# Attention output rows: from wide rows with a sum to narrow rows in four column groups

## The chip, the cores and the metric

One Trainium2 chip, one of its cores. The metric is the device time of one execution in microseconds. The time before is 189.49 us, the median of three runs (189.31 to 189.62).

## What is computed

One token (a vector x of 512) goes through an attention block with a cache and through a small MLP, and a scalar gate mixes the two. Cut to what matters:

```python
q = (x @ wq)                                   # 512 -> 32 heads of 128
s = einsum(q, k_cache) * 128 ** -0.5           # 32 heads, 4096 cached keys each
p = softmax(s)
o = einsum(p, v_cache)                         # 32 heads of 128
a = o.reshape(1, 1, 4096) @ wo                 # 4096 -> 512
b = square(relu(x @ w1 + b1)) @ w2 + b2        # 512 -> 1376 -> 512
g = sigmoid((x * gate_w).sum())
out = g * a + (1 - g) * b                      # 512 numbers, bf16
```

The caches of keys and values are 32 MB each, wq and wo 4 MB each. All inputs are bf16.

## The kernel before, in words

**Loads.** SyncE (SP) issues almost all loads, from one list in program order: wq (lines 247 and 248), the keys and values in eight pieces each of 4 MB for four heads (`load_k`, `load_v`, lines 255 to 290), w1 and w2 in between, and last wo. A load into a buffer that is used again first waits for the engines that read the buffer. wo comes in four loads (line 293), by rows `TS = [0, 20, 28, 31, 32]`: rows 0 to 19, 20 to 27, 28 to 30 and row 31 (a "row" t here is 128 rows of the matrix wo, one on each partition, 512 columns). Each load has a semaphore of its own. After them SP waits for the result (line 295) and issues the store (line 296).

**Heads.** For each piece of keys, POOL and VectorE (DVE) form products of keys and query for a part of the keys (lines 313, 680) and DVE sums them (lines 689, 695); for the other part TensorE (PE) transposes keys (line 427), ScalarE (ACT) copies the transposes (line 341) and PE forms the scores (line 441). The softmax runs on ACT (line 358), and PE multiplies by the values (line 470) into the PSUM bank `pO`. The result is copied to `pvf` (line 364, the last one line 739 on DVE), and line 479 extracts the heads into columns 288 to 415 of the bank `pX`.

**MLP.** It runs during the first piece. Its bias is put into the result rows `accs` (line 520), its output rows go to `pO` with four rows of partial sums (line 528), which are copied to `pvf` (line 380) and summed into `accs` (line 535), all long before the end.

**The end.** After the last piece, `regroup` (line 541) brings the attention result to one column per row of wo, and DVE copies it to `o2` (line 744). Then `attn_rows(c)` (line 546) runs for the four loads of wo. The result of 512 numbers lies in `accs` (line 165): two rows of 128 numbers for even column blocks (partitions 32 and 33 of the bank `pX`) and two for odd ones (partitions 0 and 1). Rows 0 to 15 of wo are wide: one matmul of 512 columns each, to partition 0, 32, 64 or 96 of `pO`, so that four partial sums arise (line 551). DVE copies these to `pvf` (line 746), and `wide_rows` (line 566) sums them into `accs`, after the first load's rows and before the second's. Rows 16 to 31 are narrow: four matmuls of 128 columns each (line 557). Which of the two partitions of a pair a matmul adds to is chosen by its stationary operand of two columns, one of which is zero; for that, `o2p` holds each column of `o2` with a zero column on either side, and `pick2` a column of the selection with zeros beside it. `busy` (line 573) issues filler matmuls whose result nobody reads. At the end DVE copies one half of the result to `ob` (line 748) and ACT the other (line 385), and SP stores two rows of 256 numbers.

Of the kernel before, what the change touches and what calls it, by code (L numbers as in the profile page):

```python
# [5 lines left out]
def bass_gated_mix__gqa_block_cached__dense_activation_squared_relu__decode_kernel(  # L6
# [14 lines left out]
    fp32 = mybir.dt.float32  # L21
    i32 = mybir.dt.int32
    bf16 = mybir.dt.bfloat16
    ALU = mybir.AluOpType
    ACT = mybir.ActivationFunctionType
    AX = mybir.AxisListType

    NH = 32
# [39 lines left out]

    TS = [0, 20, 28, 31, 32]
    NW = len(TS) - 1  # L70
    WW = 16


    k_p = A_k_cache.rearrange("a h (q b) d -> (a h q) (b d)", b=NB)
# [2 lines left out]
    wo_v = A_wo.rearrange("(p t) n -> p (t n)", t=32)  # L77
    w1_v = B_w1.rearrange("(p t) n -> p (t n)", t=4)
    w2_v = B_w2[0:F0, :].rearrange("(p g) n -> p (g n)", g=FG)
    out_v = out[0, 0, :].rearrange("(j p) -> j p", p=256)  # L80
    w2_x = B_w2[F1:F, :].rearrange("(q t) n -> q (t n)", t=TX)

    ctx = ExitStack()
    with ctx:
        def sb(name, shape, dt):
            return ctx.enter_context(nc.sbuf_tensor(name, shape, dt))
# [4 lines left out]
        def sem(name):  # L91
            return ctx.enter_context(nc.semaphore(name))
# [8 lines left out]
        wo_sb = WO.rearrange("p (t n) -> p t n", t=32)  # L101
        kT = sb("kT", [128, NR, TC * 128], bf16)
# [9 lines left out]
        grow = sb("grow", [1, DM], bf16)  # L112
        b1r = sb("b1r", [1, F], bf16)

        ob = kT[:, 1, 0:256]
        xcol = sb("xcol", [128, 4], bf16)
        sel = sb("sel", [NH, 4, 128], bf16)
        oT = sb("oT", [NH, 128], bf16)
        o2p = sb("o2p", [128, NH, 3], bf16)
        o2 = o2p[:, :, 1]  # L120
        ident = sb("ident", [128, 128], bf16)
        identf = sb("identf", [128, 128], fp32)
        pick = sb("pick", [128, 4, 60], fp32)
        pvf = sb("pvf", [112, 512], fp32)
# [20 lines left out]
        b2r = Kt[0:1, 2, 14 * 1024:14 * 1024 + DM]  # L145
        b2g = Kt[0:1, 2, 15 * 1024:16 * 1024].bitcast(fp32)

        pick2 = sb("pick2", [112, 3], fp32)

        TT = pb("T", [128, NT * 512], fp32)  # L150
        T = [TT[:, i * 512:(i + 1) * 512] for i in range(NT)]
# [2 lines left out]
        pO = pb("pO", [128, 512], fp32)  # L154
        pM = pb("pM", [128, 512], fp32)
        pX = pb("pX", [128, 512], fp32)
# [5 lines left out]
        SL = pS[0:NH, 0:256].bitcast(bf16)  # L162
        H = pX[:, 160:160 + FN + TX]

        accs = [pX[32:34, 0:128], pX[0:2, 0:128]]
        O = pX[0:NH, 288:416]

        QT = pX[:, :].bitcast(bf16).rearrange("p (j d) -> p j d", d=128)
# [66 lines left out]
        s_wm = sem("s_wm")  # L235
        s_hw = sem("s_hw")
        s_mc = sem("s_mc")
        s_wc = sem("s_wc")
        s_ww = sem("s_ww")
        s_hv = sem("s_hv")  # L240
        s_hs = sem("s_hs")
        s_acc = sem("s_acc")
        s_fin = sem("s_fin")
        s_out = sem("s_out")
# [8 lines left out]
        @on(nc.sync)  # L253
        def _(eng):
            def load_k(i):
                if i >= NK:
                    eng.wait_ge(s_t, CB[i - NK + 1])
                    eng.wait_ge(s_mu, XP * (i - NK + 1))
                    eng.wait_ge(s_pm, GP * (i - NK + 1))  # L259
                if i == 2:  # L260
                    eng.wait_ge(s_ml, 1)
                eng.dma_start(Kt[:, i % NK, :], k_p[i * 128:(i + 1) * 128, :]).then_inc(s_k[i % NK], 16)

            def load_v(i):
                if i == 1:
                    eng.wait_ge(s_qr, NQ)
                    eng.wait_ge(s_h, 2)
                if i < NQ - 2:
                    if i >= NV:
                        eng.wait_ge(s_pv, i - NV + 1)  # L270
                    eng.dma_start(VT(i), v_p[i * 128:(i + 1) * 128, :]).then_inc(s_v[i % NV], 16)
                    return
                eng.wait_ge(s_t, CB[i])
                eng.wait_ge(s_mu, XP * i)
                eng.wait_ge(s_pm, GP * i)
                eng.dma_start(VT(i), v_p[i * 128:(i + 1) * 128, :]).then_inc(s_vl[i - (NQ - 2)], 16)  # L276

            load_k(0)
            eng.dma_start(w1_sb, w1_v).then_inc(s_w1, 16)
            eng.dma_start(w2a, w2_v).then_inc(s_w2, 16)  # L280
            for r in range(4):
                eng.dma_start(WX[r:QX:4, :], w2_x[r:QX:4, :]).then_inc(s_w2, 16)
            load_k(1)
            load_v(0)
            load_k(2)
            for i in range(NQ):
                if i >= 1:
                    load_v(i)
                if i + LAG < NQ:
                    load_k(i + LAG)  # L290
            eng.wait_ge(s_pv, NQ - 3)
            for c in range(NW):
                eng.dma_start(WO[:, TS[c] * DM:TS[c + 1] * DM], wo_v[:, TS[c] * DM:TS[c + 1] * DM])\  # L293
                   .then_inc(s_wo[c], 16)
            eng.wait_ge(s_fin, 2)
            eng.dma_start(out_v, ob[32:34, :]).then_inc(s_out, 16)
            eng.wait_ge(s_out, 16)

        @on(nc.gpsimd)
# [19 lines left out]
        def _(eng):  # L319
# [46 lines left out]
            for i in range(NQ + 1):  # L366
# [14 lines left out]
                if i >= 1:  # L381
                    neg_max(i - 1)
                    exps(i - 1)
            eng.wait_ge(s_acc, 1)
            eng.activation(ob[32:34, 128:256], accs[1], ACT.Copy).then_inc(s_fin, 1)

        @on(nc.tensor)
        def _(eng):
            eng.wait_ge(s_id, 2)
            for c in range(4):  # L390
                mm = eng.transpose(SL[:, c * 128:c * 128 + 128], ident[:, c:128:4], ident[:, :])
            mm.then_inc(s_sl, 1)
            eng.wait_ge(s_x, 32)
            for t in range(4):
                mm = eng.matmul(XC[:, t:t + 1], xrow[:, t:DM:4], ident[0:1, 0:1], start=True, stop=True)
# [117 lines left out]
            def mlp_out():  # L513
                eng.wait_ge(s_w2, 16 * 5)
                eng.wait_ge(s_hs, 1)

                eng.wait_ge(s_wm, 3)
                eng.wait_ge(s_g, 4)
                for j in range(4):
                    eng.matmul(accs[j % 2], pick2[0:1, 1 - j // 2:3 - j // 2], b2g[:, j * 128:j * 128 + 128],  # L520
                               start=(j < 2), stop=False, skip_group_check=True)
                for n in range(FN + TX):
                    if n < FG:
                        rhs = w2a[0:height(n), n * DM:(n + 1) * DM]
                    else:
                        rhs = WX[:, (n - FN) * DM:(n - FN + 1) * DM]
                    r = 32 * (n % 4)
                    mm = eng.matmul(pO[r:r + 1, :], hs[0:height(n), n:n + 1], rhs, start=(n < 4),
                                    stop=(n >= FN + TX - 4))
                mm.then_inc(s_ml, 1)  # L530

            def mlp_cols():
                eng.wait_ge(s_mc, 1)
                for j in range(4):
                    eng.matmul(accs[j % 2], pick2[:, 1 - j // 2:3 - j // 2], pvf[0:112, j * 128:j * 128 + 128],
                               start=False, stop=False, skip_group_check=True)

            def regroup():
# [7 lines left out]
            def attn_rows(c):  # L546
                eng.wait_ge(s_wo[c], 16)
                for t in range(TS[c], TS[c + 1]):
                    r = 32 * (t % 4)
                    if t < WW:  # L550
                        mm = eng.matmul(pO[r:r + 1, :], o2[:, t:t + 1], wo_sb[:, t, :], start=(t < 4),
                                        stop=(t >= WW - 4), skip_group_check=True)
                        if t == WW - 1:
                            mm.then_inc(s_ww, 1)
                        continue
                    for j in range(4):
                        mm = eng.matmul(accs[j % 2], o2p[:, t, 1 - j // 2:3 - j // 2],  # L557
                                        wo_sb[:, t, j * 128:(j + 1) * 128], start=False,
                                        stop=(t == 31), skip_group_check=True)
                if c == NW - 1:  # L560
                    mm.then_inc(s_acc, 1)

            def wide_rows():
                eng.wait_ge(s_wc, 1)
                for j in range(4):
                    eng.matmul(accs[j % 2], pick2[:, 1 - j // 2:3 - j // 2], pvf[:, j * 128:(j + 1) * 128],
                               start=False, stop=False, skip_group_check=True)

            def busy(n):
                for u in range(n):
                    eng.matmul(T[0][:, :], ident[:, :], kT[:, 0, 0:512], start=True, stop=True,
                               skip_group_check=True)
# [39 lines left out]
            regroup()  # L614
            busy(2)
            for c in range(NW):
                if c == 1:
                    busy(1)
                    wide_rows()
                attn_rows(c)  # L620

        @on(nc.vector)
        def _(eng):
# [9 lines left out]
                              identf[:, :].rearrange("p (c r) -> p c r", c=4)[:, :, 0:16]  # L633
                              .rearrange("p c (b h) -> p b h c", b=4), AX.X, ALU.add).then_inc(s_ho, 1)
            eng.memset(E[:, :, :, :], 0.0).then_inc(s_ho, 1)
            eng.memset(pick2[:, :], 0.0).then_inc(s_wm, 1)
            eng.memset(o2p[:, :, :], 0.0).then_inc(s_wm, 1)
            eng.wait_ge(s_ho, 7)
            eng.wait_ge(s_wm, 2)
            eng.tensor_copy(pick2[:, 1:2], pick[0:112, 0, 28:29]).then_inc(s_wm, 1)  # L640
            eng.wait_ge(s_sl, 1)
            eng.tensor_copy(sel[:, :, :], SL.rearrange("h (c m) -> h c m", c=4)).then_inc(s_ho, 1)
            eng.wait_ge(s_x, 32)
# [98 lines left out]
            eng.tensor_scalar(oT[:, :], O, gcol[0:NH, 0:1], rden[:, 0:1], ALU.mult, ALU.mult).then_inc(s_oc, 1)  # L742
            eng.wait_ge(s_o2, 1)
            eng.tensor_copy(o2[:, :], T[1][:, 0:NH]).then_inc(s_o2, 1)
            eng.wait_ge(s_ww, 1)
            eng.tensor_copy(pvf[:, :], pO[0:112, :]).then_inc(s_wc, 1)
            eng.wait_ge(s_acc, 1)
            eng.tensor_copy(ob[32:34, 0:128], accs[0]).then_inc(s_fin, 1)  # L748


# [26 lines left out]
```

## Time and profile before

| what | value |
|---|---|
| runs | 189.49 us median, 189.31 to 189.62 |
| profiled execution: its own time | 189.48 us |
| its span in the trace | 188.2 us (1.28 us lie around it) |
| PE, DVE, ACT, POOL busy | 58%, 81%, 37%, 73% of the span |
| transfers | 78.48 MB, mean 417 GB/s |
| granted TensorE clock, mean | 0.70 of full speed |
| first load of wo issued | 149.36 us |
| first matmul that reads wo | 182.61 us |
| last matmul over | 186.65 us |
| store issued | 187.00 us |

Each line of a timeline gives the start and the length in microseconds, the engine, the line of the kernel, the operation with the tile it writes and the tile it reads, partitions x elements, and how often it occurs in the piece; behind it, in brackets, the idle time of the engine before it and what ended that. PEld is PE's loading of the stationary operand. "SPq" and "DMA" are SP's issue of a transfer and the transfer itself. A length of several instructions runs from the first start to the last end, and neighbours overlap where the array works on several at a time.

### The profile page before, as it was taken

The page shows a single profiled execution, that of the slowest core. Times are in us where ns is not written, and L with a number is a line of the kernel's source. Part 1 is how long each engine was busy: PE and PEld are TensorE (multiplying, and loading weights), DVE is VectorE, ACT ScalarE, POOL GpSimd, SP SyncE. Part 2 cuts the span into 40 slices and gives each one's busy share as a digit, 9 for nine tenths or more (in the row PEclk, how much of TensorE's full clock was granted, in tenths as well). Part 3 has the DMA queues.
Part 4 walks back from the last instruction along what each step waited for, and adds up shares of the span by engine and source line. Part 5 has one row for each costly group of instructions (what it writes and reads, how often), then busy time and mean ns, then how long its engine had stood idle before and what let it go on. Part 6 is the DMA issues. An engine that isn't in the chain of part 4 may idle for free. (4 is left out here: it accounts for less than half of the span.)

```text
span 188.2 us, 2612 instructions
## 1 busy us (share of the span) xinstructions
PE 109.7 (58%) x1076; PEld 66.2 (35%) x1078; DVE 152.9 (81%) x127; ACT 69.7 (37%) x170; POOL 137.8 (73%) x38
## 2 busy tenths in 40 slices
PE   1129877787303869146806681858282648458766
PEld 1103352437103628132704181418140634213334
DVE  7112659999997999999999999999999999991022
ACT  3003484208420829404920573055405460506000
POOL 1000199998996999989998999999899989940000
PEclk9999997857655555858665555555557585858999
DMA  7999899999999999999999999999999999999993
GB/s 265 419 432 446 375 438 438 446 425 446 430 432 439 413 425 435 425 446 432 428 425 425 432 439 421 446 432 418 432 428 432 439 425 446 421 418 424 428 394 122
DMA packets 3518, 78.48 MB, mean 417 GB/s; under 512 B 410, under 2 KB 543, under 8 KB 820
## 3 DMA queue, kind: packets, MB, share of 16 engines
q1 hardware_dynamic: 3500, 78.32, 97.3%
q8 instruction: 8, 0.13, 0.3%
q14 instruction: 2, 0.02, 0.0%
q10 hardware_dynamic: 8, 0.01, 0.0%
HBM read 78.33 MB, written 0.00 MB: 416 GB/s over the span
## 5 line engine op out<-in xcount | busy, mean ns | idle before, releaser
L313 POOL TENSOR_TENSOR pg<-Kt,qb 128x2176 f32<-128x2176 bf16 x32 | 137.1, 4317 | 28.4 <-DMA Kt<-in_A_k_cache_dram 23.3
L695 DVE TENSOR_REDUCE Sb<-pg 128x17 f32<-128x2176 f32 x32 | 77.0, 2405 | 2.2 <-POOL pg L313 2.2
L427 PE MATMUL T<-ident,Kt 128*128 128x128 bf16 x256 | 27.6, 294 | 19.2 <-DMA Kt<-in_A_k_cache_dram 19.2
L341 ACT ACTIVATE kT<-T 128x1024 bf16<-128x1024 bf16 x32 | 30.8, 1030 | 17.5 <-PE T L427 17.4
L680 DVE TENSOR_TENSOR pr<-Kt,pQ 128x1792 f32<-128x1792 bf16 x16 | 32.2, 2011 | 1.9 <-DMA Kt<-in_A_k_cache_dram 1.1
L427 PEld LDWEIGHTS T<-ident,Kt 128*128 128x128 bf16 x256 | 24.0, 137 | 23.8 <-DMA Kt<-in_A_k_cache_dram 22.1
L689 DVE TENSOR_REDUCE Sb<-pr 128x14 f32<-128x1792 f32 x16 | 32.1, 2004 | 0.0
L470 PE MATMUL pO<-Vt,E 128*16 128x512 bf16 x192 | 23.0, 576 | 0.5 <-issue 0.5
L358 ACT ACTIVATE E<-Sb,nM 32x128 bf16<-32x128 f32 x32 | 18.7, 583 | 0.9
L351 ACT ACTIVATE nM<-pM 128x4 f32<-128x4 f32 x8 | 1.4, 173 | 46.5 <-PE pM L455 46.5
L441 PE MATMUL pS<-qc,kT 128*128 128x4 bf16 x256 | 11.9, 168 | 8.5 <-ACT kT L341 8.4
L412 PE MATMUL T<-Vt,kT 128*128 128x512 bf16 x32 | 10.0, 454 | 7.8 <-DMA Vt<-in_A_wq_dram 7.8
L451 PE MATMUL pM<-identf,mp 128*1 128x128 f32 x8 | 2.9, 359 | 19.3 <-DVE mp L702 19.3
L441 PEld LDWEIGHTS pS<-qc,kT 128*128 128x128 bf16 x256 | 10.4, 104 | 10.2 <-ACT kT L341 10.1
L479 PE MATMUL pX<-pvf,pick 112*32 112x128 f32 x64 | 12.8, 366 | 1.8 <-ACT pvf L364 1.8
L667 DVE CAST qb<-T 32x128 bf16<-32x128 f32 x12 | 3.4, 287 | 9.2 <-PE T L412 8.9
L333 ACT ACTIVATE qb<-T 32x128 bf16<-32x128 f32 x20 | 5.4, 268 | 14.3 <-PE T L412 13.9
L479 PEld LDWEIGHTS pX<-pvf,pick 112*32 112x32 f32 x64 | 8.6, 146 | 5.2 <-ACT pvf L364 2.5
L470 PEld LDWEIGHTS pO<-Vt,E 128*16 128x16 bf16 x192 | 6.6, 108 | 7.3 <-issue 5.7
L358 ACT ACTIVATION_READ_ACCUMULATOR E<-Sb,nM 32x1 f32 x32 | 8.2, 257 | 0.0
L451 PEld LDWEIGHTS pM<-identf,mp 128*1 128x1 f32 x8 | 0.6, 80 | 20.8 <-DVE mp L702 20.6
L455 PE MATMUL pM<-gm,onesf 1*128 1x4 f32 x16 | 4.1, 322 | 6.5 <-DVE gm L706 6.5
(81 smaller groups left out, 76.3 us busy)
## 6 DMA issues: line engine op xcount, KB each, us to landing
Kt<-in_A_k_cache_dram SPq DMA_DIRECT2D x8, 4096.0 KB, 31.2
Vt<-in_A_v_cache_dram SPq DMA_DIRECT2D x6, 4096.0 KB, 31.0
Kt<-in_A_v_cache_dram SPq DMA_DIRECT2D x2, 4096.0 KB, 31.6
Vt<-in_A_wq_dram SPq DMA_DIRECT2D x1, 3840.0 KB, 11.8
Vt<-in_A_wo_dram SPq DMA_DIRECT2D x1, 2560.0 KB, 33.2
Kt<-in_B_w_dram SPq DMA_DIRECT2D x1, 1376.0 KB, 23.9
Kt<-in_B_w_dram SPq DMA_DIRECT2D x1, 1280.0 KB
Vt<-in_A_wo_dram SPq DMA_DIRECT2D x1, 1024.0 KB, 35.2
```

The costliest lines, as they stand in the source:

```text
L313: eng.tensor_tensor(pg[:, n % 2, 0:g, :], Kt[:, i % NK, k * g * 128:(k + 1) * g * 128] .rearrange("p (b d) -> p b d", b=g), qb[:, i:i + 1, ...
L333: eng.activation(qb[a:b, j, :], T[j % NT][a:b, h * 128:(h + 1) * 128], ACT.Copy)\
L341: eng.activation(kT[:, n % NR, :], T[n % NT][:, :].bitcast(bf16), ACT.Copy).then_inc(s_ev, 1)
L358: eng.activation(E[a:b, j % NE, :, h], Sb[a:b, j % NS, :], ACT.Exp, bias=nM[a:b, 4 * j + h:4 * j + h + 1], scale=SCALE, accum_out=RS[a:b, ...
L412: mm = eng.matmul(T[j % NT][:, :], xb[:, t, :], wq_sb[:, t, j * 512:(j + 1) * 512], start=(t == 0), stop=(t == 3))
L427: mm = eng.transpose(T[n % NT][:, :].bitcast(bf16)[:, y * 128:(y + 1) * 128], Kt[:, i % NK, w * 128:(w + 1) * 128], ident[:, :])
L441: mm = eng.matmul(S[:, c * TC + y, :], kT[:, n % NR, y * 128:(y + 1) * 128], qc[:, 4 * i:4 * i + 4], start=True, stop=True)
L470: mm = eng.matmul(pO[r:r + 16, :], E[:, i % NE, 4 * y:4 * y + 4, :], VT(i)[:, y * 512:(y + 1) * 512], start=(y < 4), stop=(y >= NG - 4))
L479: mm = eng.matmul(O, pick[0:112, b, 28 - 4 * i:60 - 4 * i], pvf[:, b * 128:(b + 1) * 128], start=False, stop=(i == NQ - 1 and b == 3), ski ...
L680: eng.tensor_tensor(pr[:, 0:x, :], Kt[:, i % NK, a * 128:(a + x) * 128] .rearrange("p (b d) -> p b d", b=x), PQ[:, i % 4:i % 4 + 1, :].bro ...
L689: eng.tensor_reduce(Sb[:, i % NS, a:a + x], pr[:, 0:x, :], AX.X, ALU.add).then_inc(s_sd, 1)
L695: eng.tensor_reduce(Sb[:, i % NS, k * g:(k + 1) * g], pg[:, n % 2, 0:g, :], AX.X, ALU.add)\
```

## The change

All 32 rows of wo become narrow. The result lies in four single rows, one for each block of 128 columns, at partitions 0, 32, 64 and 96 of `pX`, so that each of the four matmuls of a row of wo goes to a column group of its own. The stationary operand has one column; `o2p` with its zero columns and the zero columns of `pick2` go, and with them two memsets. The wide rows, DVE's copy of their sums, the sum and one filler matmul go. At the end DVE copies 97 partitions of 128 numbers in one instruction, ACT copies nothing, and SP stores four rows of 128 numbers after one event in place of two.

```diff
-    WW = 16
-    out_v = out[0, 0, :].rearrange("(j p) -> j p", p=256)
+    out_v = out[0, 0, :].rearrange("(j p) -> j p", p=128)
-        ob = kT[:, 1, 0:256]
+        ob = kT[:, 1, 0:128]
-        o2p = sb("o2p", [128, NH, 3], bf16)
-        o2 = o2p[:, :, 1]
+        o2 = sb("o2", [128, NH], bf16)
-        pick2 = sb("pick2", [112, 3], fp32)
+        pick2 = sb("pick2", [112, 1], fp32)
-        accs = [pX[32:34, 0:128], pX[0:2, 0:128]]
+        accs = [pX[32 * j:32 * j + 1, 0:128] for j in range(4)]
...
-            eng.wait_ge(s_fin, 2)
-            eng.dma_start(out_v, ob[32:34, :]).then_inc(s_out, 16)
+            eng.wait_ge(s_fin, 1)
+            eng.dma_start(out_v, ob[0:97:32, :]).then_inc(s_out, 16)
...
-            eng.wait_ge(s_acc, 1)
-            eng.activation(ob[32:34, 128:256], accs[1], ACT.Copy).then_inc(s_fin, 1)
...
                 for j in range(4):
-                    eng.matmul(accs[j % 2], pick2[0:1, 1 - j // 2:3 - j // 2], b2g[:, j * 128:j * 128 + 128],
-                               start=(j < 2), stop=False, skip_group_check=True)
+                    eng.matmul(accs[j], pick2[0:1, :], b2g[:, j * 128:j * 128 + 128],
+                               start=True, stop=False, skip_group_check=True)
...
-                    eng.matmul(accs[j % 2], pick2[:, 1 - j // 2:3 - j // 2], pvf[0:112, j * 128:j * 128 + 128],
+                    eng.matmul(accs[j], pick2[:, :], pvf[0:112, j * 128:j * 128 + 128],
...
                 for t in range(TS[c], TS[c + 1]):
-                    r = 32 * (t % 4)
-                    if t < WW:
-                        mm = eng.matmul(pO[r:r + 1, :], o2[:, t:t + 1], wo_sb[:, t, :], start=(t < 4),
-                                        stop=(t >= WW - 4), skip_group_check=True)
-                        if t == WW - 1:
-                            mm.then_inc(s_ww, 1)
-                        continue
                     for j in range(4):
-                        mm = eng.matmul(accs[j % 2], o2p[:, t, 1 - j // 2:3 - j // 2],
+                        mm = eng.matmul(accs[j], o2[:, t:t + 1],
                                         wo_sb[:, t, j * 128:(j + 1) * 128], start=False,
                                         stop=(t == 31), skip_group_check=True)
...
-            def wide_rows():
-                eng.wait_ge(s_wc, 1)
-                for j in range(4):
-                    eng.matmul(accs[j % 2], pick2[:, 1 - j // 2:3 - j // 2], pvf[:, j * 128:(j + 1) * 128],
-                               start=False, stop=False, skip_group_check=True)
...
             for c in range(NW):
-                if c == 1:
-                    busy(1)
-                    wide_rows()
                 attn_rows(c)
...
-            eng.memset(pick2[:, :], 0.0).then_inc(s_wm, 1)
-            eng.memset(o2p[:, :, :], 0.0).then_inc(s_wm, 1)
             eng.wait_ge(s_ho, 7)
-            eng.wait_ge(s_wm, 2)
-            eng.tensor_copy(pick2[:, 1:2], pick[0:112, 0, 28:29]).then_inc(s_wm, 1)
+            eng.tensor_copy(pick2[:, :], pick[0:112, 0, 28:29]).then_inc(s_wm, 1)
...
-            eng.wait_ge(s_ww, 1)
-            eng.tensor_copy(pvf[:, :], pO[0:112, :]).then_inc(s_wc, 1)
             eng.wait_ge(s_acc, 1)
-            eng.tensor_copy(ob[32:34, 0:128], accs[0]).then_inc(s_fin, 1)
+            eng.tensor_copy(ob[0:97, :], pX[0:97, 0:128]).then_inc(s_fin, 1)
```

More of the change, by code (lines that the diff above doesn't have):

```diff
@@ L237, in bass_gated_mix__gqa_block_cached__dense_activation_squared_relu__decode_kernel @@
         s_mc = sem("s_mc")
-        s_wc = sem("s_wc")
-        s_ww = sem("s_ww")
         s_hv = sem("s_hv")
@@ L515, in mlp_out @@
                 eng.wait_ge(s_hs, 1)
-                eng.wait_ge(s_wm, 3)
+                eng.wait_ge(s_wm, 1)
                 eng.wait_ge(s_g, 4)
                 for j in range(4):
-                    eng.matmul(accs[j % 2], pick2[0:1, 1 - j // 2:3 - j // 2], b2g[:, j * 128:j * 128 + 128],
-                               start=(j < 2), stop=False, skip_group_check=True)
+                    eng.matmul(accs[j], pick2[0:1, :], b2g[:, j * 128:j * 128 + 128],
+                               start=True, stop=False, skip_group_check=True)
                 for n in range(FN + TX):
```

## The prediction

> **What bounds the kernel now.** I read the 40 slices first. The DMA row stands at nine tenths or more nearly from end to end, and only the last slice, 4.7 us wide, falls to 3. Whatever happens on an engine before that slice is paid for only if it delays a transfer.
>
> ```profile
> DMA  7999899999999999999999999999999999999993
> q1 hardware_dynamic: 3500, 78.32, 97.3%
> q8 instruction: 8, 0.13, 0.3%
> ```
>
> The chain of work that ended last then says which transfer hands over to which engine. These are its last pieces (start, length, what):
>
> ```profile
> 149.36 0.42 SPq L293
> 149.79 0.05 issue
> 149.84 35.22 DMA Vt<-in_A_wo_dram
> 185.05 0.04 issue
> 185.10 1.57 PE pX L557 x48
> 186.67 0.02 issue
> 186.69 0.28 DVE kT L748
> ```
>
> The piece with 35.22 us is the second of the four loads of wo, rows 20 to 27 (the first has 20 rows, the third 3, the last 1). The reader is to see that the 48 narrow matmuls start at 185.10 because this load landed at 185.06, not because the wide rows were finished then. The timeline of the last stage shows how close the two are:
>
> ```profile
> 182.61 1.03 PE L551 MATMUL pO<-Vt,o2p 128*1 128x512 bf16 x16 [0.55 <-DMA Vt<-in_A_wo_dram]
> 183.47 0.61 PE L557 MATMUL pX<-Vt,o2p 128*2 128x128 bf16 x16
> 183.69 0.69 DVE L746 COPY pvf<-pO 112x512 f32<-112x512 f32 x1 [2.30 <-PE pO L551]
> 184.01 0.39 PE L573 MATMUL T<-kT,ident 128*128 128x512 bf16 x1
> 184.44 0.61 PE L566 MATMUL pX<-pvf,pick 112*2 112x128 f32 x8
> 185.10 1.55 PE L557 MATMUL pX<-Vt,o2p 128*2 128x128 bf16 x48
> 186.69 0.28 DVE L748 CAST kT<-pX 2x128 bf16<-2x128 f32 x1 [2.31 <-PE pX L557]
> 187.00 0.29 SPq L296 DMA_DIRECT2D out_dram<-kT  x1
> ```
>
> The sum of the wide rows ends at 184.44 + 0.61 = 185.05, within 0.01 us of the landing. So the copy and the sum are covered exactly by the wait for rows 20 to 27. The loads after it set the rest. The list of DMA issues gives time to landing:
>
> ```profile
> Vt<-in_A_wo_dram SPq DMA_DIRECT2D x1, 384.0 KB, 35.7
> Vt<-in_A_wo_dram SPq DMA_DIRECT2D x1, 128.0 KB, 35.5
> ```
>
> SP issues these two at 150.31 and 150.78 (timeline of SP), so they land at about 186.01 and 186.28. The weight loads of the last row start at 186.36 in the same timeline. The row that decides the end is row 31, the one whose load comes last.
>
> **The change, part by part.**
>
> Row speed. Line 557 now alternates between two column groups. 48 matmuls take 1.55 us, one takes 219 ns (its group's mean), so (1.55 - 0.22) / 47 = 28 ns from start to start, and a row of four takes 4 x 28 = 112 ns. What four column groups do is shown by the wide rows. Asked for 182.60 to 182.64 alone, the timeline gives
>
> ```profile
> 182.61 0.39 PE L551 MATMUL pO<-Vt,o2p 128*1 128x512 bf16 x4 [0.55 <-DMA Vt<-in_A_wo_dram]
> ```
>
> Four matmuls of 378 ns lie within 0.39 us, so all four start within some 12 ns. I take the same for narrow ones: a row of four starts in 12 ns, and the next row follows after the time in which one group streams 128 columns, which is that of a pair today, 56 ns. Bounds for a row are 12 ns below and 4 x 56 = 224 ns above (no overlap at all); 56 is nearest to both the wide rows and the pairs.
> The Trainium skill, TensorE: Matmul & The Clock Gate, section "Wait — 56ns, not 53.3ns?", says that start-to-start never falls below about 25 ns. The four starts in 12 ns do not agree when the column groups differ. By the rule the first 20 rows would take 80 x 25 = 2.0 us and the last row 3 x 25 + 219 = 294 ns, and the sum below would come out about 0.06 us later.
>
> First load, rows 0 to 19. It removes 16 wide and 16 narrow matmuls, one filler matmul (0.39), DVE's copy (0.69) and 8 sums (0.61). It adds 80 narrow ones: 20 x 56 ns + 0.22 = 1.3 us, from 182.61 to 183.9. Nothing is gained: the next rows wait for 185.06 as before. What was removed is replaced by 1.2 us of waiting. The cover holds as long as 80 matmuls fit into 185.10 - 182.60 = 2.5 us, 31 ns each.
>
> Rows 20 to 30. From 185.10, eight rows take 0.45 us plus 0.22, done by 185.8; three rows from 186.04 start by 186.16. All are issued before row 31 lands, so their gain is hidden too.
>
> Row 31. Two pairs 56 ns apart become four starts in 12 ns. The end moves from 186.37 + 0.06 + 0.22 = 186.65 to 186.37 + 0.01 + 0.22 = 186.60: -0.05 us, the only gain on the path.
>
> The clock. The granted clock changes in steps of 3.41 us. Asked in those stretches (length, PE busy, then the other engines and the clock):
>
> ```profile
> 27.59:31.00 3.41, 2.19 (x33) 1.16 (x31) 3.41 (x2) 2.84 (x7) 3.41 (x1) 1.00 1.17 498
> 31.00:34.42 3.42, 3.42 (x11) 1.07 (x9) 3.42 (x3) 0.00 (x0) 3.42 (x2) 0.50 0.98 422
> 174.36:177.78 3.42, 2.51 (x31) 1.09 (x34) 0.16 (x1) 0.00 (x0) 0.00 (x0) 1.00 0.96 410
> 181.19:184.60 3.41, 2.56 (x39) 1.15 (x41) 0.90 (x2) 0.00 (x0) 0.00 (x0) 1.00 0.90 368
> ```
>
> After full-clock stretches with 2.5 us or more of PE the clock stayed; after those with 1.77 to 2.31 it fell to 0.50, one of 2.17 excepted. The new kernel has in 181.19 to 184.60 only 0.60 (fillers) + 1.29 = 1.89 us. So I expect half clock from 184.60. Then eight rows take 0.9 us from 185.10, three rows from 186.04 leave the array free at about 186.37, and row 31 takes the 314 ns that line 427's 128-column matmuls have at half clock (219 at full): 186.37 + 0.01 + 0.32 = 186.70. This is +0.05 against 186.65, in place of -0.05. Bounds: -0.05 and, if every earlier row also queues up, +0.15.
>
> Tail. Today ACT (267 ns) and DVE (283 ns) copy side by side; the change leaves one DVE copy of 97x128. DVE's 128x128 copy at line 661 takes 276 ns and the 128x32 one at line 744 215, so size hardly counts: 0, bounds -0.07 and +0.03. SP waits for one event, not two; ACT's was the earlier, so 0. SP's issue takes 286 ns for two rows and about 430 for 128 rows, so two more rows cost nothing. The store lands 0.8 us after its issue (SP's waits). Four rows of 256 bytes instead of two of 512: no row of the trace shows a 256-byte store; bounds -0.1 and +0.8 (a second landing), and I take 0 because 0.8 us for 1 KB is latency, not size.
>
> Start of the kernel. DVE loses two memsets (61 and 138 ns, at 2.8 us); PE's next need there, the q projection, waits 7.8 us for wq until 13.1, so 0. The bias and MLP column matmuls keep their number and sit under the loads: 0. The copy of o2 (215 ns at 181.18) writes densely now, and PE then waits for wo until 182.60: 0. SP's waits and loads of K, V and wo are untouched.
>
> Sum: the profiled execution is 189.48 us (span 188.2 and 1.28 around it; the median of the runs is 189.49, so it stands for them). 189.48 + 0.05 = **189.53** with the clock lost, 189.43 with it kept.
>
> **Rivals.**
> 1. The store becomes dearer (slower). Place: after 187.29, nothing covers it. If 256-byte rows need a second access of the kind that a landing is, it costs up to 0.8: 189.9 to 190.3. It decides from 0.3 us on. For: the packets are half as long and twice as many. Against: 410 of the 3518 packets of the profile are under 512 B already, and the transfer was at 417 GB/s with them.
> The Trainium skill, DMA: Bandwidth & Descriptors, section "Specifications", puts 512 bytes as the least for full rate and says that below it the engine reads, modifies and writes. The store of four rows falls under this, the store of two does not; no run so far shows what it does to one store's latency.
> 2. The groups do not run side by side for narrow rows (slower). Price: 80 x 56 = 4.5 us, from 182.60 to 187.1, then 48 x 56 = 2.7 more: the end at 189.95 instead of 186.65, 192.8 in all. It decides above 31 ns a matmul. The four starts in 12 ns speak against it.
> 3. Instruction loads shift the last landing. Queue q8 moved 8 packets, 0.13 MB, 16 KB each; at 417/16 = 26 GB/s such a packet holds one DMA engine for 0.6 us. The change adds 48 matmuls and as many weight loads to the first rows and takes away some 20 instructions, so a block boundary may fall elsewhere: 0.6 earlier (188.9) or later (190.1). Against: the program up to 182 keeps its instructions, so the boundaries before it stay.
> 4. The wide rows were on the path (faster): the next rows start early. That needs the landing at 185.06 to be an effect of PE; but SP issued that load at 149.84 without waiting for these rows. At most 0.05.
>
> **How the numbers follow.** Forecast, hidden behind the loads: 0.78, of it 0.45 with the clock lost (189.5) and 0.33 with it kept (189.4). The store dearer by over 0.3: 0.09. Groups one by one: 0.02. Instruction block later: 0.04, and earlier or another gain of over 0.4: 0.07. A measurement of this kernel can tell about 0.2% (0.38 us) from no change, so the forecast counts as the same: 0.78; slower 0.09 + 0.02 + 0.04 = 0.15; faster 0.07. Range: below 189.43 less the spread of the runs (0.18), 189.2; above, the store's bound, 190.3.
>
> **What would show it.** Right: a wait of about 1.2 us for wo before the second group of rows, with line 557's 80 matmuls in about 1.3 us; PE's last matmul between 186.55 and 186.75; DVE's last copy near 283 ns; the store 0.8 us from issue to landing. Wrong: no wait at 185 (row speed), a landing of wo at another time (instruction load), a store over 1.1 us, or a longer last copy.

## The result, and the profile after

The changed kernel takes 189.90 us (median of 9 runs, 189.78 to 190.14) against 189.41 us for the kernel before in the same comparison (9 runs, 189.31 to 189.62). The ratio is 1.0027, with a 95% interval of 1.0018 to 1.0036: slower by about 0.5 us. The profiled execution took 189.81 us, with a span of 188.4 us.

The timeline of the last stage of the changed kernel (start, length, engine, line, operation, idle time before it and what ended it; line 544 is the row matmul, 719 the last copy, 292 the store):

```profile
182.42 1.29 PE L544 MATMUL pX<-Vt,o 128*1 128x128 bf16 x80 [0.18 <-DMA Vt<-in_A_wo_dram]
...
184.93 0.62 PE L544 MATMUL pX<-Vt,o 128*1 128x128 bf16 x32 [1.22 <-DMA Vt<-in_A_wo_dram]
...
185.84 0.54 PE L544 MATMUL pX<-Vt,o 128*1 128x128 bf16 x16 [0.30 <-DMA Vt<-in_A_wo_dram]
186.15 0.09 PEld L544 LDWEIGHTS pX<-Vt,o 128*1 128x1 bf16 x4 [0.16 <-DMA Vt<-in_A_wo_dram]
186.44 0.29 DVE L719 CAST kT<-pX 97x128 bf16<-97x128 f32 x1 [4.85 <-PE pX L544]
186.75 0.59 SPq L292 DMA_DIRECT2D out_dram<-kT  x1
```

Down to the copy this is the forecast's case with the clock kept. The first 80 matmuls take 1.29 us. Then PE waits 1.22 us for rows 20 to 27, again 0.30 us for rows 28 to 30, and the weight loads of row 31 wait 0.16 us more. The last copy takes 0.29 us. The last line is the one that differs: SP's issue of the store takes 0.59 us, and it took 0.29 us before. After the issue, SP's waits show a longer landing too. The first line is of the kernel before, the second of the changed kernel (waiting line, what it waited for, total, times, longest):

```profile
SPq L297 <- DMA out_dram<-kT: 0.8, 1, 0.8
```

```profile
SPq L293 <- DMA out_dram<-kT: 1.0, 1, 1.0
```

So the store took 0.29 + 0.8 = 1.1 us before and takes 0.59 + 1.0 = 1.6 us now: +0.5 us, all behind the last engine's work, where nothing covers it. Less the 0.04 us gained at row 31 (worked out further below), that is the difference of the medians. In these two profiles the span differs by less, 0.2 us, because wo also landed 0.2 us earlier in the profile after: row 31's weight loads start at 186.15 there, and in the kernel before at 186.36:

```profile
186.36 0.10 PEld L557 LDWEIGHTS pX<-Vt,o2p 128*2 128x2 bf16 x4
```

The loads of wo are the same in both kernels. In the other profiles below with four column groups that start lies between 186.13 and 186.31, and one with the compute of before starts its last copy at 186.45 in place of 186.69, so this part is scatter between executions.

### The profile page after: what moved, and what is told of

Read it like the earlier page. It is cut to its first block, busy times and chain, and to the rows that moved or that the text cites. A ratio compares the mean times of both kernels' runs of the same rounds, so it can differ in the third digit from the quotient of the medians.

```text
span 188.4 us, 2685 instructions
## 1 busy us (share of the span) xinstructions
PE 105.0 (56%) x1115; PEld 63.5 (34%) x1117; DVE 152.0 (81%) x124; ACT 69.4 (37%) x169; POOL 137.8 (73%) x38
## 5 line engine op out<-in xcount | busy, mean ns | idle before, releaser
L421 PE MATMUL T<-ident,Kt 128*128 128x128 bf16 x256 | 25.6, 280 | 18.7 <-DMA Kt<-in_A_k_cache_dram 18.7
L421 PEld LDWEIGHTS T<-ident,Kt 128*128 128x128 bf16 x256 | 22.3, 130 | 22.9 <-DMA Kt<-in_A_k_cache_dram 21.2
L464 PE MATMUL pO<-Vt,E 128*16 128x512 bf16 x192 | 20.3, 512 | 0.4 <-issue 0.4
L473 PE MATMUL pX<-pvf,pick 112*32 112x128 f32 x64 | 14.4, 402 | 2.4 <-ACT pvf L360 2.4
L473 PEld LDWEIGHTS pX<-pvf,pick 112*32 112x32 f32 x64 | 9.5, 160 | 5.9 <-ACT pvf L360 2.9
```

Of the source, the lines that this page charges most:

```text
L421: mm = eng.transpose(T[n % NT][:, :].bitcast(bf16)[:, y * 128:(y + 1) * 128], Kt[:, i % NK, w * 128:(w + 1) * 128], ident[:, :])
L464: mm = eng.matmul(pO[r:r + 16, :], E[:, i % NE, 4 * y:4 * y + 4, :], VT(i)[:, y * 512:(y + 1) * 512], start=(y < 4), stop=(y >= NG - 4))
L473: mm = eng.matmul(O, pick[0:112, b, 28 - 4 * i:60 - 4 * i], pvf[:, b * 128:(b + 1) * 128], start=False, stop=(i == NQ - 1 and b == 3), ski ...
```

## The experiments

Theory A was formed from these lines: the dear part is the store, because its four rows lie 32 partitions apart (called A1 where only the store is in question). Three rivals stood beside it. A2: the four rows of 256 bytes might cost the time, not their distance. C: the ninth packet of instructions, which the page of the profile after has and the one before has not ("q8 instruction: 9" against 8), might hold up the store. D: the compute part of the change might cost the time, and the store be longer by chance. Where a kernel below stores other rows than its result rows, it leaves out the right result, and only its time is of use.

### The store of the kernel before on the compute of the kernel after

```diff
-    out_v = out[0, 0, :].rearrange("(j p) -> j p", p=128)
+    out_v = out[0, 0, :].rearrange("(j p) -> j p", p=256)
...
-        ob = kT[:, 1, 0:128]
+        ob = kT[:, 1, 0:256]
...
-            eng.dma_start(out_v, ob[0:97:32, :]).then_inc(s_out, 16)
+            eng.dma_start(out_v, ob[0:2, :]).then_inc(s_out, 16)
...
-            eng.tensor_copy(ob[0:97, :], pX[0:97, 0:128]).then_inc(s_fin, 1)
+            eng.tensor_copy(ob[0:97, 0:128], pX[0:97, 0:128]).then_inc(s_fin, 1)
```

> The kernel after with the store of the kernel before: two rows of 512 bytes from two neighbouring partitions (what it stores is not the result; columns 128 to 255 hold old data). Theory A, the store of four rows 32 partitions apart costs it all (issue 586 against 286 ns, first packet 0.16 us later): SP's issue back at about 290 ns, 0.8 us from issue's end to landing, and 0.05 faster than the kernel before, 189.35, ratio 0.9997. Rival C, the ninth instruction packet that runs from 186.10 to 187.23 delays the store: the packet is still there, so no change, 189.9, ratio 1.0027.

Measured: 189.34 us (189.22 to 189.53, 11 runs) against 189.37 (189.21 to 189.61) for the kernel before, ratio 1.0000 (0.9991 to 1.0009). The timeline's end and the queue of instructions:

```profile
186.53 0.29 DVE L719 CAST kT<-pX 97x128 bf16<-97x128 f32 x1 [4.84 <-PE pX L544]
186.85 0.29 SPq L292 DMA_DIRECT2D out_dram<-kT  x1
```

```profile
q8 instruction: 9, 0.15, 0.3%
```

The issue is back at 0.29 us and the time with it, while all the compute of the change is in place and the ninth instruction packet is still there. Rival C falls: the packet is there and costs nothing here. The rest of the change (column groups, no wide rows, one copy of 97 partitions) is worth nothing that the runs can tell; the interval leaves 0.17 us either way.

### The store of the kernel after on the compute of the kernel before

```diff
-    out_v = out[0, 0, :].rearrange("(j p) -> j p", p=256)
+    out_v = out[0, 0, :].rearrange("(j p) -> j p", p=128)
...
-            eng.dma_start(out_v, ob[32:34, :]).then_inc(s_out, 16)
+            eng.dma_start(out_v, ob[0:97:32, 0:128]).then_inc(s_out, 16)
```

> The kernel before with the store of the kernel after alone: four rows of 256 bytes, 32 partitions apart (what it stores is not the result). Theory A: issue 586 ns, and 0.45 to 0.5 slower than the kernel before, 189.9, ratio 1.0025. Rival C: there is no ninth instruction packet, so no change, 189.41. Rival D, the compute part of the change costs the time: no change here, 189.41.

Measured: 189.84 us (189.71 to 189.98, 9 runs), ratio 1.0025 (1.0015 to 1.0035). The compute is that of before, and there are 8 instruction packets:

```profile
184.84 1.56 PE L557 MATMUL pX<-Vt,o2p 128*2 128x128 bf16 x48
...
186.45 0.28 DVE L748 CAST kT<-pX 2x128 bf16<-2x128 f32 x1 [2.30 <-PE pX L557]
186.76 0.58 SPq L296 DMA_DIRECT2D out_dram<-kT  x1
```

The store alone brings the whole loss. Rivals C and D fall by this run also.

### Four rows from neighbouring partitions

The kernel after, with another store.

```diff
-            eng.dma_start(out_v, ob[0:97:32, :]).then_inc(s_out, 16)
+            eng.dma_start(out_v, ob[0:4, :]).then_inc(s_out, 16)
```

> The kernel after, but the four rows of 256 bytes come from partitions 0 to 3 in place of 0, 32, 64 and 96 (what it stores is not the result). Theory A1, the distance of the partitions costs the time: issue about 290 ns, 189.4, ratio 0.9998. Theory A2, the number of rows or their 256 bytes cost it: issue 586 ns, 189.9, ratio 1.0027.

Measured: 189.41 us (189.20 to 189.76, 11 runs), ratio 1.0004 (0.9995 to 1.0013).

```profile
186.79 0.30 SPq L292 DMA_DIRECT2D out_dram<-kT  x1
```

Four rows of 256 bytes cost 0.30 us to issue, two of 512 cost 0.29. Neither the number of rows nor their length is dear.

### Two rows of 512 bytes, 32 partitions apart

The kernel before, with another store.

```diff
-            eng.dma_start(out_v, ob[32:34, :]).then_inc(s_out, 16)
+            eng.dma_start(out_v, ob[32:65:32, :]).then_inc(s_out, 16)
```

> The kernel before, its two rows of 512 bytes stored from partitions 32 and 64 in place of 32 and 33 (the second row stored is not the result). Theory A1, distance: issue above 400 ns and 189.6 to 189.9. Theory A2, number or size of rows: issue 286 ns, 189.41, ratio 1.0000.

Measured: 189.77 us (189.69 to 189.93, 11 runs), ratio 1.0022 (1.0013 to 1.0031).

```profile
186.98 0.59 SPq L296 DMA_DIRECT2D out_dram<-kT  x1
```

Two rows apart cost as much as four rows apart, 0.59 us. In these runs the price goes by the step between the rows and is paid once, not by the row.

### Four rows, two partitions apart

The kernel after, with another store.

```diff
-            eng.dma_start(out_v, ob[0:97:32, :]).then_inc(s_out, 16)
+            eng.dma_start(out_v, ob[0:7:2, :]).then_inc(s_out, 16)
```

> The kernel after with its four rows stored from partitions 0, 2, 4 and 6 (what it stores is not the result). If any step other than 1 is dear: issue about 586 ns, 189.9, ratio 1.0025. If only rows in different groups of 32 partitions are dear: issue about 300 ns, 189.4.

Measured: 190.03 us (189.87 to 190.10, 6 runs) against 189.43 (189.29 to 189.63), ratio 1.0030 (1.0019 to 1.0041).

```profile
186.91 0.66 SPq L292 DMA_DIRECT2D out_dram<-kT  x1
```

All four rows lie in the same group of 32 partitions now, and the issue is as dear or dearer. What counts in these runs is whether the step between partitions is 1. The landing goes the same way: SP's waits show 1.0 us after the issue in all four profiles of stores with a step of 2 or 32, and 0.8 or 0.9 us in all others.

### The wide rows alone

The kernel before with all 32 rows narrow in its two column groups; its result rows and its store stay.

```diff
-    WW = 16
+    WW = 0
...
             for c in range(NW):
-                if c == 1:
-                    busy(1)
-                    wide_rows()
                 attn_rows(c)
...
-            eng.wait_ge(s_ww, 1)
-            eng.tensor_copy(pvf[:, :], pO[0:112, :]).then_inc(s_wc, 1)
```

> The kernel before with all 32 rows narrow in two column groups, no wide rows, no copy and sum; its result rows and store of two neighbouring rows stay. Theory A, the wait for the second load of wo takes the place of what is removed, and the store alone costs the time: 80 matmuls at 28 ns are over by about 184.9, before that load lands, so no change, 189.37, ratio 0.999 to 1.001. Rival D, the wide rows' removal itself costs or gains: more than 0.2 either way.

Measured: 189.42 us (189.37 to 189.67, 11 runs) against 189.43 (189.29 to 189.63), ratio 1.0001 (0.9993 to 1.0010).

```profile
182.82 2.21 PEld L557 LDWEIGHTS pX<-Vt,o2p 128*2 128x2 bf16 x80 [0.49 <-DMA Vt<-in_A_wo_dram]
...
185.31 1.34 PEld L557 LDWEIGHTS pX<-Vt,o2p 128*2 128x2 bf16 x48 [0.28 <-DMA Vt<-in_A_wo_dram]
```

The 80 weight loads of the first rows are over at 185.03, the next group's begin at 185.31 after 0.28 us of waiting for wo. Even at 28 ns a matmul the wide rows, their copy and their sum can go without a trace in the time: the landing of the next rows takes their place.

### A repair with the full result

```diff
-    out_v = out[0, 0, :].rearrange("(j p) -> j p", p=128)
+    out_v = out[0, 0, :].rearrange("(j p) -> j p", p=512)
...
-        ob = kT[:, 1, 0:128]
+        ob = kT[:, 1, 0:512]
...
-            eng.wait_ge(s_fin, 1)
-            eng.dma_start(out_v, ob[0:97:32, :]).then_inc(s_out, 16)
+            eng.wait_ge(s_fin, 4)
+            eng.dma_start(out_v, ob[0:1, :]).then_inc(s_out, 16)
...
+            eng.wait_ge(s_acc, 1)
+            for j in (1, 3):
+                eng.activation(ob[0:1, j * 128:j * 128 + 128], accs[j], ACT.Copy).then_inc(s_fin, 1)
...
-            eng.tensor_copy(ob[0:97, :], pX[0:97, 0:128]).then_inc(s_fin, 1)
+            for j in (0, 2):
+                eng.tensor_copy(ob[0:1, j * 128:j * 128 + 128], accs[j]).then_inc(s_fin, 1)
```

> A repair of the kernel after with the full result: four copies of 1x128 into one partition, two on VectorE and two on ScalarE side by side, and a store of one row of 1 KB. Theory A: the store's issue falls to 210 to 290 ns, the second copy on each engine adds 0.2 to 0.27, so 189.34 + 0.2 = 189.55, between the two kernels, ratio 1.001.

Measured: 189.66 us (189.58 to 189.80, 11 runs) against 189.43, ratio 1.0012 (1.0003 to 1.0020).

```profile
186.52 0.60 DVE L723 CAST kT<-pX 1x128 bf16<-1x128 f32 x2 [5.25 <-PE pX L547]
187.15 0.28 SPq L292 DMA_DIRECT2D out_dram<-kT  x1
```

The issue falls to 0.28 us, but two copies of 1x128 take 0.60 us where one of 97x128 takes 0.29. The repair gives back about half of the 0.5 us and stays 0.23 us behind the kernel before, a little more than expected (189.55 forecast, 189.66 measured): the second copy adds 0.31 us, not 0.2 to 0.27.

### The fillers and the clock

The compute of the kernel after with the store of two neighbouring rows (its edits as above), and no filler matmul at all.

```diff
...
             def busy(n):
-                for u in range(n):
+                for u in range(0):
```

> The kernel after with the store of two neighbouring rows (not the result) and without any filler matmul, to see the clock step of the prediction. If the clock falls to half for the last stage as the prediction had it: last rows at 112 ns, end 0.1 later at the least, 189.45, and up to 190.3 if the stage before wo's first load becomes slow enough to use up its wait. If the clock stays at 1.00: 189.34.

Measured: 189.95 us, from 189.33 to 190.45 in 12 runs; ratio 1.0026 (1.0013 to 1.0040). The median hides two groups: six runs lie between 189.33 and 189.65, six between 190.25 and 190.45, and none between them. The runs of every other kernel here stay within 0.6 us. The mean granted clock of a run does not tell the groups apart (0.655 to 0.681 in the short ones, 0.665 to 0.710 in the long ones). The profiled execution took 189.43 us and is one of the short ones; its granted clock was (length, PE, PEld, DVE, ACT and POOL busy, clock):

```profile
175.30:178.70 3.40, 2.38 (x24) 0.93 (x28) 0.00 (x0) 0.00 (x0) 0.00 (x0) 0.50 1.03 440
182.10:185.50 3.40, 2.13 (x116) 1.69 (x116) 0.36 (x2) 0.00 (x0) 0.00 (x0) 1.00 0.83 331
```

At half clock the last 32 matmuls by the values take 3.59 us, where the kernel after takes 1.90 us for them at full clock. So the copy of `o2` ends at 182.82, later than the first load of wo lands, and PE starts on the rows at 182.87 behind VectorE:

```profile
176.31 3.59 PE L464 MATMUL pO<-Kt,E 128*16 128x512 bf16 x32 [1.98 <-issue]
...
182.63 0.19 DVE L717 CAST o<-T 128x32 bf16<-128x32 f32 x1 [0.35 <-PE T L535]
182.87 1.10 PEld L544 LDWEIGHTS pX<-Vt,o 128*1 128x1 bf16 x80 [0.39 <-DVE o L717]
...
186.13 0.09 PEld L544 LDWEIGHTS pX<-Vt,o 128*1 128x1 bf16 x3 [0.16 <-DMA Vt<-in_A_wo_dram]
186.37 0.08 PEld L544 LDWEIGHTS pX<-Vt,o 128*1 128x1 bf16 x1 [0.16 <-issue]
```

Without fillers the wait before wo's first load is used up. In this execution that does not reach the end, because PE still waits 0.76 us for the second load. The rows of wo themselves ran at full clock (1.00 from about 180.6 to 187.2), so the prediction's case of half clock there is not seen. The last two lines show something else: the fourth weight load of row 31 starts 0.24 us after the first three, and nothing in the profile says what it waited for. What makes six of the runs 0.8 us longer was not shown; the clock is likely, but no long run has a profile.

## Why the prediction was right and where it failed

**Right: the wait takes the place of the wide rows.** The waits of 1.22 and 0.30 us for wo and the unchanged times of both partial kernels (ratios 1.0000 and 1.0001) show it.

**Right: row speed.** 80 matmuls took 1.29 us (1.3 forecast), so four column groups run side by side for narrow rows. Rival 2 is out. The rule of the Trainium skill (TensorE: Matmul & The Clock Gate, "Wait — 56ns, not 53.3ns?") of at least about 25 ns from start to start would have made it 2.0 us; across different column groups the trace disagrees: (1.29 - 0.22) / 79 = 13.5 ns.

**Right: the gain of row 31.** From the start of its weight loads to the start of the last copy it is 186.69 - 186.36 = 0.33 us before and 186.44 - 186.15 = 0.29 us after: 0.04 us earlier, with 0.05 forecast. In the time it can't be told from nothing.

**Wrong: the clock.** The forecast of half clock from 184.60, and with it +0.05 in place of -0.05, did not come true. The clock stayed at 1.00 in the profile after:

```profile
182.10:185.50 3.40, 2.00 (x113) 1.53 (x112) 0.00 (x0) 0.00 (x0) 0.00 (x0) 1.00 0.84 336
185.50:188.00 2.50, 0.58 (x20) 0.24 (x16) 0.29 (x1) 0.00 (x0) 0.00 (x0) 1.00 0.03 8
```

Two things were off. The clock's last rise lies at about 175.25 in this profile and at 170.95 in that of before; counted on in steps of 3.41 us, the steps end at 185.5 here, not at 184.60. The place of the steps had been taken from one execution and does not carry over to another. And PE's busy time alone does not decide: this stretch had 2.0 us, within the 1.77 to 2.31 us after which I expected a fall, and the clock stayed, while in the same profile it fell after a full-clock stretch with 2.28 us (28.48 to 31.89). The exception among the rows of before (2.17 us, and the clock stayed) should have kept both cases even. What decides is open. The error was worth 0.1 us.

**Wrong: the tail, the step that failed.** The prediction said: "SP's issue takes 286 ns for two rows and about 430 for 128 rows, so two more rows cost nothing." The interpolation was over the number of rows, and the runs show that the number does not matter (0.30 us for four neighbours). The change also altered the step between partitions from 1 to 32, and that costs 0.3 us at the issue and about 0.2 until the landing, with two rows and with four. The prediction's own sign of being wrong, a store over 1.1 us, came, counted from the start of the issue to the landing: 1.6 us. The trace of before even had a row for such a step. The four small loads of w2's rest go to every fourth partition (`WX[r:QX:4, :]`, five rows each), and the profile of before gives their issue times, here behind one of the loads to 128 neighbouring partitions:

```profile
2.12 0.43 SPq L279 DMA_DIRECT2D Kt<-in_B_w_dram  x1
...
L282 SPq DMA_DIRECT2D Kt<-in_B_w_dram x4: 657/672/809, 3.2 to 5.5; - x4
```

Five rows take 672 ns where 128 neighbouring rows take 430. These are loads and not a store, but taken as the nearest row they would have put 0.67 - 0.29 = 0.38 us on the issue, and the sum at 189.43 + 0.38 = 189.8.

**Rival 1 had the place, not the mechanism.** It put the loss behind the last copy, where nothing covers it, up to 0.8 us; measured 0.5. But it blamed the length of the rows. The rule of the Trainium skill that it named (DMA: Bandwidth & Descriptors, "Specifications", 512 bytes) does not show in one store's time: four rows of 256 bytes from neighbouring partitions gave a ratio of 1.0004 (0.9995 to 1.0013), which leaves room for 0.25 us at most; their landing took 0.9 us against 0.8.

**Rival 3 (instruction packets).** A ninth packet did come, as it might, but after the changed compute it lies beside a time that is unchanged (189.34 us). It moved nothing. By the row of queue q8 (0.3% of the span of 16 engines for 9 packets) a packet holds an engine for about 1 us, an estimate, and not for the 0.6 us of the prediction.

**The number and the range.** The forecast of no change that can be told, 0.78, was too sure: one cost without a row of its own was set to 0 where the bounds reached to +0.8. The sum of 189.53 us was 0.37 us short, and the loss of 0.49 us is more than the 0.38 us that the prediction itself called tellable. That 189.90 us lies in the range of 189.2 to 190.3 is owed to the upper bound of rival 1, whose mechanism was not the one at work; so far it was luck.

## What to carry to other kernels

When a store or load changes shape, compare its access pattern with transfers of the same pattern in the trace, not with those of the same size: here a step of 2 or 32 between partitions cost 0.3 us at the issue, and at the end of a kernel that is paid in full. Work that is done inside a wait for a transfer may be removed without any effect on the time, as the wide rows here; look first at which event ends the wait, and at whether the work also keeps up the clock, as the run without fillers warns. And let the layout of the result be chosen from the store backwards: here the layout with four column groups gained 0.04 us at row 31 and cost 0.5 us at the store.

## What the runs showed of the hardware

A transfer from SBUF whose rows lie on partitions with a step of 2 or 32 took SP 0.58 to 0.66 us to issue, one from neighbouring partitions or a single one 0.28 to 0.30 us; with two rows or four it is the same. The landing after the issue also came later, 1.0 us against 0.8 to 0.9. Narrow matmuls (128x128 with one stationary column) that go to four column groups in turn started 13.5 ns apart, those to two groups (two stationary columns) 28 ns. Two copies of 1x128 from PSUM in a row took 0.60 us on VectorE, twice one of 97x128 (0.29 us): one copy of 1 partition took 0.28 us, as long as one of 97, and the second came wholly behind the first.
